# Decay rows of two half batches in own tiles, added by three-row matmuls, in a fused attention and gated FFN kernel

## Chip, cores, metric

One Trainium2 chip, one core. The metric is the device time of one execution in microseconds (us). Runs of the kernel before spread over about 1% (271.16 to 272.87 us in the first three). A run is marked slow when it is over 1.5% above the fastest run of the same kernel. The experiments ran on four chips; each run is compared with the kernel before on its own chip, in the same rounds.

## The reference, cut

```python
def _attn_ref(q, k, v, f):                     # q, k, v: (8, 8, 576, 64); f: (8, 8, 576)
    scores = scale * q @ k^T
    cum = np.cumsum(np.log(np.clip(f, 0.0001, 1.0)), axis=-1)
    decay = cum[:, :, :, None] - cum[:, :, None, :]
    scores = np.where(causal, -1e9, scores + decay)
    ... softmax ...
    return attn @ v
def _moe_ref(x, w_in, conv_w, w_out):          # x: (8, 576, 512), d_ff 1024
    h = np.maximum(x @ w_in, 0.0)
    ... three-tap convolution along the sequence, gate = sigmoid(conv) ...
    return (h * gate) @ w_out
```

The decay is of low rank. It can be added to q·k by a few additional rows in the contraction: rows that hold cum of the key beside a constant, and a constant beside cum of the query. cum is kept as a bf16 pair (high, low), which makes three rows.

## The kernel before, the parts concerned

The work is cut in 16 half batches of four heads ("hb"). q and k of a half batch lie transposed in 128-row tiles `stq`, `stk`. The decay rows are rows 96, 98 and 126 of these same tiles, so one 128-row matmul gives q·k and decay together. Before that, VectorE "clamps" each tile: one pass multiplies every row by a constant and adds another, so it can keep a row or set it to a constant. After the scores come the exponential (ScalarE), attention times V into a PSUM buffer "O" (TensorE), and a normalisation by the row sums (VectorE); V is cast to fp16 beforehand. The FFN then uses the weights W_in and W_out. The order of all instructions on every engine is fixed beforehand: the host plays through a list of tasks with estimated times and priorities (the third argument).

```python
def fill(t, p0, n, z):                  # constant rows of a tile, copied by DMA
    nc.gpsimd.dma_start(bass.AP(... n rows from p0 ...), consts[z:z + n, :])

def rows_of(hb):                        # decay rows, by DMA into the q and k tiles
    tq, tk = stq_t[hb % RING], stk_t[hb % RING]
    c = slice(hb * HH, (hb + 1) * HH)
    if hb == 1:
        nc.gpsimd.dma_start(tk[96:97, 0:HS], khi_sb[c, :])
        nc.gpsimd.dma_start(tk[98:99, 0:HS], klo_sb[c, :])
        nc.gpsimd.dma_start(tq[126:127, 0:HS], khi_sb[c, :])
        return
    ...

def scores(sc, hb, k0, q0, w, start=True, stop=True):
    nc.tensor.matmul(sc, stk_t[hb % RING][:, k0:k0 + 128], stq_t[hb % RING][:, q0:q0 + w],
                     start=start, stop=stop, skip_group_check=True)
...
            if hb:                      # q, k loaded: constant fills (GpSimd), clamp (VectorE)
                even.append(task({"POOL": 0.55 * len(rows)}, [t_fsrc, x], 2 * hb - 3.5, ... fill ...))
            if hb and (s or hb < CLAMPS):
                even.append(task({"DVE": 0.9}, [x], (2 * hb - 3 if hb > 1 else -5) + 0.2 * s, ... clamp(hb, s, 0, 4, 96)))
...
        if hb:
            t_rows[hb] = even + [task({"POOL": 1.1 if hb > 1 else 1.6}, landed, ..., rows_of(hb), lag=LANDING + 1.0)]
...
            t_norm[i] = task({"DVE": 1.05}, [t_pv[i, 1]], i - 0.0, lambda i=i: norm(i) if i else [norm(i), hold(w_in_f16)], ...)
            if i == 0:                  # W_in is loaded only after the first normalisation
                t_win = task({"POOL": 1.0}, [t_norm[0]], -0.5, ... dma_start(w_in_f16, ...) ...)
```

## Time and profile before

| | before |
|---|---|
| median of 3 runs | 271.61 us (271.16 to 272.87) |
| span of the profiled run | 271.1 us |
| TensorE busy | 241.7 us (89%), 2602 matmuls |
| VectorE / ScalarE busy | 226.9 / 212.1 us |

These are lines of the page of the kernel before: the busy share of TensorE and its granted clock in 40 slices of 6.8 us (tenths), and the group of score matmuls (count, busy us, mean ns of one, idle time before them).

```profile
PE   2864869878899999999999999999999999989990
...
PEclk9999868999999999999999999999999999999997
...
L298 PE MATMUL sc<-stq,stk 128*128 128x128 bf16 (+3 forms) x576 | 67.3, 242 | 8.1 <-ACT pm L338 3.6
```

After the start, TensorE has its gaps in slices 3 to 11 (and again at the very end), and its clock is low in slices 5 to 7. That is the stretch that the change aims at.

### The profile page before, as it was taken

What the parts mean: (1) busy time and instruction counts of PE and PEld (TensorE: products, weight loads), DVE (VectorE), ACT (ScalarE), POOL (GpSimd) and SP (SyncE); (2) the same over time, 40 slices, a digit from 0 to 9 for tenths busy, and PEclk for the clock granted to TensorE, in tenths of its full rate; (3) what the DMA queues carried; (4) which work ended last, traced back from release to release, by engine and by line L of the source; (5) the groups of instructions that cost most, each with busy time, mean ns of one, the idle gap of its engine ahead of it and who ended that gap; (6) DMA issues with size and microseconds to landing.
All of it is one profiled execution on the core that took longest, in us unless ns stands there. A gap on an engine that the chain in (4) does not pass through costs nothing.

```text
span 271.1 us, 6621 instructions
## 1 busy us (share of the span) xinstructions
PE 241.7 (89%) x2602; PEld 166.1 (61%) x2602; DVE 226.9 (84%) x401; ACT 212.1 (78%) x347; POOL 59.2 (22%) x124
## 2 busy tenths in 40 slices
PE   2864869878899999999999999999999999989990
PEld 1333646646677777776776677667776777655540
DVE  5863538999799999999989989999899999978751
ACT  5081727989879999989989899989889998577552
POOL 4491110631120340332315050406010100000000
PEclk9999868999999999999999999999999999999997
DMA  8999999999998999999999999999101201022015
GB/s 138 202 209 177 223 184 221 222 183 246 168 220 183 219 244 166 228 167 256 269 213 180 203 245 185 223 160 278 61 28 52 80 0 58 23 116 80 0 46 226
DMA packets 121284, 44.58 MB, mean 164 GB/s; under 512 B 115560, under 2 KB 116596, under 8 KB 121254
## 3 DMA queue, kind: packets, MB, share of 16 engines
q1 hardware_dynamic: 115088, 32.00, 66.9%
q0 software_dynamic: 5840, 12.01, 17.0%
q8 instruction: 20, 0.33, 0.5%
q10 hardware_dynamic: 326, 0.17, 0.4%
q14 instruction: 10, 0.08, 0.1%
HBM read 13.99 MB, written 9.58 MB: 87 GB/s over the span
## 4 chain that ended last, share of the span: by engine, by line
PE 64%; DVE 8%; DMA 7%; issue 6%; SPq 6%; ACT 5%; POOL 0%; DVEq 0%; ACTq 0%; POOLq 0%
PE mm L425 19%; PE mm L487 19%; PE sc L298 10%; PE O L356 8%; DMA stk<-in_k_dram 6%; SPq L110 5%; PE sc L330 4%; DVE u L457 2%; PE sc L500 2%; PE mm L393 2%; DVE u L455 2%; SPq L163 1%; ACT ht L438 1%; DMA out_dram<-ob 1%; ACT po L324 1%
## 5 line engine op out<-in xcount | busy, mean ns | idle before, releaser
L425 PE MATMUL mm<-xt,w_in_f 128*128 128x288 f16 x512 | 80.3, 292 | 1.7 <-DVE xt L413 0.4
L298 PE MATMUL sc<-stq,stk 128*128 128x128 bf16 (+3 forms) x576 | 67.3, 242 | 8.1 <-ACT pm L338 3.6
L324 ACT ACTIVATE po<-sc 128x1024 f16<-128x1024 f32 x64 | 64.6, 1028 | 2.6 <-PE sc L298 2.1
L438 ACT ACTIVATE ht<-mm 128x288 f16<-128x288 f32 x128 | 52.0, 414 | 12.3 <-PE mm L425 11.2
L298 PEld LDWEIGHTS <-stk 128*128 128x128 bf16 x576 | 42.4, 99 | 28.7 <-issue 7.7
L425 PEld LDWEIGHTS <-w_in_f 128*128 128x128 f16 x512 | 48.2, 100 | 18.7 <-issue 3.1
L487 PE MATMUL mm<-w_out_f,hg 128*128 128x512 f16 x248 | 58.4, 379 | 0.7 <-ACT xt L411 0.6
L455 DVE SCALAR_TENSOR_TENSOR u<-ht,cwt 128x576 f32<-128x576 f16 x64 | 51.5, 810 | 5.4 <-ACT ht L438 4.7
L457 DVE SCALAR_TENSOR_TENSOR u<-ht,cwt,u 128x576 f32<-128x576 f16 x64 | 51.5, 810 | 0.5
L475 DVE SCALAR_TENSOR_TENSOR hg<-hg,ht 128x576 f16<-128x576 f16 x56 | 41.6, 751 | 4.4 <-ACT hg L467 4.0
L467 ACT ACTIVATE hg<-u,cwt 128x576 f16<-128x576 f32 x56 | 43.4, 780 | 1.0 <-DVE u L457 0.9
L338 ACT ACTIVATE pm<-sc 128x1024 f16<-128x1024 f32 x32 | 32.9, 1028 | 11.8 <-PE sc L298 11.7
L487 PEld LDWEIGHTS <-hg 128*128 128x128 f16 x248 | 23.5, 98 | 24.2 <-issue 0.9
L356 PE MATMUL O<-va,po 128*128 128x65 f16 x640 | 36.6, 194 | 1.2 <-ACT po L324 1.0
L356 PE MATMUL O<-va,pm 128*128 128x65 f16 x256 | 31.1, 194 | 3.0 <-DVE xn L369 1.8
L356 PEld LDWEIGHTS <-po 128*128 128x128 f16 x640 | 30.5, 97 | 2.4 <-ACT po L324 1.8
L356 PEld LDWEIGHTS <-pm 128*128 128x128 f16 x256 | 24.1, 98 | 5.7 <-DVE xn L369 2.7
L369 DVE TENSOR_TENSOR xn<-O,rc 128x640 f16<-128x640 f32 x32 | 26.4, 824 | 1.1
L132 POOL DMA_DIRECT2D stq<-consts x23 | 12.2, 535 | 66.8 <-PE mm L425 27.0
L330 PE MATMUL sc<-trib,identb 128*128 128x512 bf16 x64 | 24.5, 383 | 1.2 <-ACT po L324 1.1
L511 ACT ACTIVATE ob<-mm 128x512 f32<-128x512 f32 x23 | 13.7, 598 | 11.0 <-PE mm L487 10.7
L522 POOL DMA_DIRECT2D out_dram<-ob x10 | 7.7, 768 | 44.2 <-ACT ht L438 21.9
(112 smaller groups left out, 223.8 us busy)
## 6 DMA issues: line engine op xcount, KB each, us to landing
vf<-in_v_dram SPq DMA_DIRECT2D x64, 128.0 KB, 4.0
out_dram<-ob POOLq DMA_DIRECT2D x10, 512.0 KB, 6.4
out_dram<-ob SPq DMA_DIRECT2D x10, 256.0 KB, 2.1
stq<-consts POOLq DMA_DIRECT2D x8, 216.0 KB, 4.7
vf<-in_v_dram SPq DMA_DIRECT2D x16, 64.0 KB, 5.2
w_in_f<-in_moe_w_in_dram POOLq DMA_DIRECT2D x1, 1024.0 KB, 10.7
w_out_f<-in_moe_w_out_dram POOLq DMA_DIRECT2D x4, 256.0 KB, 5.6
out_dram<-ob SPq DMA_DIRECT2D x2, 512.0 KB, 2.8
```

What stands on the lines that cost most here:

```text
L298: nc.tensor.matmul(sc, stk_t[hb % RING][:, k0:k0 + 128], stq_t[hb % RING][:, q0:q0 + w], start=start, stop=stop, skip_group_check=True)
L324: nc.scalar.activation(p_of[i, s][:, 0:1024], sc_of.pop((i, s)), AF.Exp, scale=SCALE)
L330: nc.tensor.matmul(sc[:, 512 * s:512 * (s + 1)], identb, trib, start=True, stop=False, skip_group_check=True)
L338: nc.scalar.activation(p_of[i, 2], sc_of.pop((i, 2)), AF.Exp, scale=SCALE)
L356: nc.tensor.matmul(O[:, s, 65 * Q:65 * (Q + 1)], w, va[:, h, m, :], start=(m == 0), stop=(m == Q))
L425: nc.tensor.matmul(ps[:, 0:w], w_in_f16[:, cc, 128 * ff:128 * (ff + 1)], xt[:, cc, w * t:w * (t + 1)], start=(cc == 0), stop=(cc == NCC - 1))
L438: nc.scalar.activation(ht[:, 0, HT_0 + w * t:HT_0 + w * (t + 1)], ps[:, 0:w], AF.Relu)
L455: nc.vector.scalar_tensor_tensor(u, hl, cwt[:, ff, 0:1], hc, op0=ALU.mult, op1=ALU.add)
L457: nc.vector.scalar_tensor_tensor(u, hr, cwt[:, ff, 1:2], u, op0=ALU.mult, op1=ALU.add)
L467: nc.scalar.activation(hv, u, AF.Tanh, scale=cwt[:, ff, 2:3])
L475: nc.vector.scalar_tensor_tensor(hv, hv, 1.0, hc, op0=ALU.add, op1=ALU.mult)
L487: nc.tensor.matmul(ps, chunk(g, ff, c), w_out_f16[:, ff, :], start=(ff == 0), stop=(ff == NFF - 1))
```

## The change

Its intent: half batches 1 and 2 no longer wait for decay rows in their q and k tiles. Their decay rows lie in tiles of their own, borrowed from buffers that are needed only later (V of batch 1; x^T and u), and each of their 36 score matmuls is followed by one over these three rows into the same accumulator. In addition, TensorE gets 20 matmuls of 512 columns in gaps after half batches 0 and 1, and priorities are set anew. Core of the diff (cuts marked by ...):

```diff
+    def decay_rows(hb, dk, dq):
+        dec_of[hb] = dk, dq
+        nc.gpsimd.memset(dk.bitcast(FP32), MINUS)
+        nc.gpsimd.memset(dq.bitcast(FP32), PAIR)
+    def load_decay(hb):
+        (dk, dq), c = dec_of[hb], slice(HH * hb, HH * (hb + 1))
+        nc.gpsimd.dma_start(dk[0:1, 0:HS], khi_sb[c, :])
+        nc.gpsimd.dma_start(dk[1:2, 0:HS], klo_sb[c, :])
+        nc.gpsimd.dma_start(dq[2:3, 0:HS], khi_sb[c, :])
...
+    decay_rows(1, early[0:3, 0:HS // 2].bitcast(BF16), early[0:3, HS // 2:HS].bitcast(BF16))
+    decay_rows(2, xt_pool.tile(...)...[0:3].bitcast(BF16), u_pool.tile(...)...[0:3].bitcast(BF16))
...
+    load_decay(1)
+    load_decay(2)
...
+    def warm():
+        ps = mm_pool.tile([128, 512], FP32, name="mm")
+        for t in range(2):
+            nc.tensor.matmul(ps, identb, trib, start=True, stop=True)
...
         nc.tensor.matmul(sc, stk_t[hb % RING][:, k0:k0 + 128], stq_t[hb % RING][:, q0:q0 + w],
-                         start=start, stop=stop, skip_group_check=True)
+                         start=start, stop=stop and hb not in dec_of, skip_group_check=True)
+        if hb in dec_of:
+            dk, dq = dec_of[hb]
+            n = min(128, HS - k0)
+            nc.tensor.matmul(sc[0:n], dk[0:3, k0:k0 + n], dq[0:3, q0:q0 + w],
+                             start=False, stop=stop, skip_group_check=True)
...
-    CLAMPS, HALVES, LANDING = 8, 16, 3.0
+    CLAMPS, HALVES, LANDING = 6, 8, 3.0
-    WAITS = ((3, 0), (3, 1), (4, 0), (4, 1))
+    WAITS = ((3, 1), (3, 1), (4, 0), (4, 1))
+    WARM = {0: 5, 1: 5}
...
-            t_norm[i] = task({"DVE": 1.05}, [t_pv[i, 1]], i - 0.0, ...
+            t_norm[i] = task({"DVE": 1.05}, [t_pv[i, 1]], i - 1.5, ...
...  (V loads of the next batches wait for half batch 1's scores; FFN keys, AHEAD, QUEUED set anew)
```

More of the change, by code (lines that the diff above doesn't have):

```diff
@@ L138, in rows_of @@
         c = slice(hb * HH, (hb + 1) * HH)
-        if hb == 1:
-            nc.gpsimd.dma_start(tk[96:97, 0:HS], khi_sb[c, :])
-            nc.gpsimd.dma_start(tk[98:99, 0:HS], klo_sb[c, :])
-            nc.gpsimd.dma_start(tq[126:127, 0:HS], khi_sb[c, :])
-            return
         nc.gpsimd.dma_start(tq[126:127, 0:HS], kd[0:1, c, :].rearrange("j h s -> j (h s)"))
@@ L147, in rows_of @@
                             kd[:, c, :].rearrange("j h s -> j (h s)"))
+    dec_of = {}
+    def decay_rows(hb, dk, dq):
[7 more added lines that the diff above has]
+        nc.gpsimd.dma_start(dq[2:3, 0:HS], khi_sb[c, :])
     def hold(w):
@@ L208 @@
     nc.gpsimd.tensor_copy(trv, trib[:, 0:SL].unsqueeze(1).broadcast_to((128, HH, SL)))
+    early = vf_t[1].rearrange("p h k d -> p (h k d)")
+    decay_rows(1, early[0:3, 0:HS // 2].bitcast(BF16), early[0:3, HS // 2:HS].bitcast(BF16))
+    decay_rows(2, xt_pool.tile([128, NCC, S], FP16, name="xt").rearrange("p c s -> p (c s)")[0:3].bitcast(BF16),
+               u_pool.tile([128, 2, S], FP32, name="u").rearrange("p a s -> p (a s)")[0:3].bitcast(BF16))
     nc.vector.memset(one1, 1.0)
@@ L558 @@
     last = None
+    t_dec = {hb: task({"ACT": 0.01}, [], -99, lambda: None, lag=x) for hb, x in ((1, 4.5), (2, 6.0))}
+    t_held = task({"ACT": 0.01}, [], -99, lambda: None, take="xt", also="u")
     t_fsrc = task({"DVE": 3.1}, [], -9, fill_sources)
@@ L572 @@
                 landed.append(x)
-            if hb:
+            if hb > 2:
                 t = (stq_t, stk_t)[s][hb % RING]
@@ L579 @@
             if hb and (s or hb < CLAMPS):
-                even.append(task({"DVE": 0.9}, [x], (2 * hb - 3 if hb > 1 else -5) + 0.2 * s,
-                                 lambda hb=hb, s=s: clamp(hb, s, 0, 4, 96)))
+                even.append(task({"DVE": 0.9}, [x], (2 * hb - 2 if hb > 1 else -5) + 0.2 * s,
+                                 lambda hb=hb, s=s: clamp(hb, s, 0, 4, 96 if hb > 2 else 128)))
         t_half = None
         if b == 0 and hb < 2:
-            t_half = task({"ACT": 0.01}, [], -9, lambda: None, lag=(6.5, 9.3)[hb])
+            t_half = task({"ACT": 0.01}, [], -9, lambda: None, lag=(7.5, 12.0)[hb])
             t_v[b] = t_half
         elif hb < HALVES:
-            last = t_half = task({"SP": 3.2}, [t_cast[hb - 4, p] for p in range(2)] if b >= 2 else [], key + 0.2,
+            last = t_half = task({"SP": 3.2}, [t_cast[hb - 4, p] for p in range(2)] if b >= 2 else
+                                 t_qk[1, 0] + t_qk[1, 1], key + 0.2,
                                  lambda b=b, h=HH * (hb % 2): load_v(b, h, h + HH), lag=2.3, dma=3.0, behind=last)
         elif hb % 2 == 0:
-            last = t_v[b] = task({"SP": 3.5}, [t_cast[2 * b - j, p] for j in (4, 3) for p in range(2)] if b >= 2 else [],
+            last = t_v[b] = task({"SP": 3.5}, [t_cast[2 * b - j, p] for j in (4, 3) for p in range(2)] if b >= 2 else
+                                 t_qk[1, 0] + t_qk[1, 1],
                                  key + 1.2, lambda b=b: load_v(b), lag=2.3, dma=6.0, behind=last)
@@ L596 @@
         if hb:
-            t_rows[hb] = even + [task({"POOL": 1.1 if hb > 1 else 1.6}, landed, 2 * hb - 3.6 if hb > 1 else -9 if hb > 1 else -1.0,
-                                      lambda hb=hb: rows_of(hb), lag=LANDING + 1.0)]
+            t_rows[hb] = even + [task({"POOL": 1.1}, landed, 2 * hb - 3.6, lambda hb=hb: rows_of(hb), lag=LANDING + 1.0)
+                                 if hb > 2 else t_dec[hb]]
         else:
@@ L616 @@
             exps = {}
-            x = task({"PE": 0.9}, t_rows[hb], i + 0.1, lambda i=i: diag_scores(i), take="sc")
+            x = task({"PE": 1.33 if hb in t_dec else 0.9}, t_rows[hb], i + 0.1, lambda i=i: diag_scores(i), take="sc")
             t_qk[hb, p] = [t_tail, x]
@@ L620 @@
             for s in range(2):
-                x = task({"PE": 0.46}, t_rows[hb], i + 0.2 + 0.4 * s, lambda i=i, s=s: off_scores(i, s),
+                x = task({"PE": 0.89 if hb in t_dec else 0.46}, t_rows[hb], i + 0.2 + 0.4 * s, lambda i=i, s=s: off_scores(i, s),
                          take="sc")
@@ L630 @@
                                   give=[("pm", mask)] if s else [])
-            t_norm[i] = task({"DVE": 1.05}, [t_pv[i, 1]], i - 0.0, lambda i=i: norm(i) if i else [norm(i), hold(w_in_f16)],
+            t_norm[i] = task({"DVE": 1.05}, [t_pv[i, 1]], i - 1.5, lambda i=i: norm(i) if i else [norm(i), hold(w_in_f16)],
                              take="xn" if i % PPB == 0 else None, give=[("O", t_pv[i, 0])])
@@ L635 @@
                     w_in_f16, moe_w_in.rearrange("(cc p) ff -> p cc ff", p=128)), lag=2.0, dma=6.5)
+        if hb == 2:
+            task({"ACT": 0.01}, t_qk[2, 0] + t_qk[2, 1], -9, lambda: None, give=[("xt", t_held), ("u", t_held)])
+        if hb in WARM:
+            x = None
+            for _ in range(WARM[hb]):
+                x = task({"PE": 0.44}, [t_pv[2 * hb + 1, 1], x], 999, warm, take="mm", lag=0.05)
+                gives = tasks[x][4]
+                gives.append(("mm", x))
         if hb % 2:
@@ L644 @@
             t_xt[b].append(task({"DVE": 0.3, "ACT": 0.4}, [x], i, lambda e, b=b: xpose_out(b, "t", 0, e), give=[("mm", x)]))
-    start = [PPB * (b0 + nb) + 1.0 for b0, nb in GROUPS]
-    start += [start[-1] + 4.0, start[-1] + 6.0]
+    start = [PPB * (b0 + nb) + x for (b0, nb), x in zip(GROUPS, (-1.0, 1.0, 1.5, 1.0, 1.0, 1.5, 1.5, 1.0))]
+    start += [PPB * B + 5.0, PPB * B + 7.0]
     t_exp, t_late = [], []
@@ L654 @@
         for ff in range(NFF):
-            key = start[g] + 0.8 * (start[g + 1] - start[g]) * ff / NFF
+            key = start[g] + .8 * (start[g + 1] - start[g]) * ff / NFF
             relus = []
@@ L699 @@
             t_m2.append(x)
-            x = task({"DVE": 0.62, "ACT": 0.57}, [x] + ([y] if c % 2 else []), key - 1.0,
+            x = task({"DVE": 0.62, "ACT": 0.57}, [x] + ([y] if c % 2 else []), key - 4.0,
                      lambda e, g=g, c=c: evac(g, c, e), give=[("mm", x)] if g < LAST else [], take="ob" if c % 2 == 0 else None)
@@ L709 @@
             task({"SP": 0.01}, t_m2, key, lambda: None, give=[("hg", t_hg)])
-    AHEAD, QUEUED = 3.0, 8.0
+    AHEAD, QUEUED = 8.0, 6.0
     def play():
@@ L715, in play @@
         ready = {e: [] for e in busy}
-        dma_free, clock = 21.5, 0.0
+        dma_free, clock = 23.0, 0.0
         heap, order = [], []
```

## The prediction

> **What bounds the kernel now.** I read the busy shares by stretch first, then the waits between 18 and 80 us, then the order of time of the early part engine by engine, last the DMA issues and their landings. The stretches (columns: PE, PE weight load, DVE, ACT, POOL busy us with counts, granted clock, DMA share, GB/s):
>
> ```profile
> 18.00:25.00 7.00, 3.01 (x65) 2.40 (x65) 2.38 (x7) 1.98 (x3) 3.44 (x6) 1.00 1.13 166
> 25.00:38.00 13.00, 9.80 (x128) 7.40 (x128) 7.14 (x21) 6.64 (x8) 2.03 (x4) 0.80 1.20 207
> 38.00:44.00 6.00, 5.67 (x30) 3.69 (x30) 3.20 (x7) 2.96 (x7) 0.50 (x1) 0.58 1.11 232
> 44.00:50.00 6.00, 5.69 (x77) 4.44 (x76) 5.12 (x10) 6.00 (x10) 0.79 (x2) 1.00 1.17 202
> 50.00:70.00 20.00, 15.25 (x206) 11.02 (x203) 19.86 (x36) 18.02 (x29) 8.27 (x14) 1.00 1.21 211
> 80.00:100.00 20.00, 19.93 (x226) 14.21 (x224) 18.95 (x31) 18.27 (x30) 4.75 (x9) 1.00 1.00 206
> ```
>
> There are three regimes. Up to 44 us nothing is full: TensorE waits, and from 25 to 44 us its clock is low too. From 50 to 70 us VectorE is full (19.86 of 20) and TensorE has nearly 5 us to spare. From 70 to about 250 us TensorE is full (19.93 of 20 here, the same in each later stretch up to 220 us). So what the early part loses is never made up: it pushes a nearly full pipeline to the right. Time is to be had before 70 us and nowhere else; the last 11 us (PE 4.88) are a tail that the change leaves alone.
>
> What ends the idle time early, as the order of time shows it:
>
> ```profile
> 25.07 0.28 PE L298 MATMUL sc<-stq,stk 128*128 128x64 bf16 x4 [2.69 <-DMA stq<-khi_sb]
> ```
> ```profile
> 24.72 0.43 DVE L170 TENSOR_SCALAR va<-vf 128x512 f16<-128x512 f32 x1 [3.63 <-DMA vf<-in_v_dram]
> 35.10 0.88 DVE L119 TENSOR_SCALAR stk<-stk,lim 96x2304 uint16<-96x2304 uint16 x1 [1.21 <-DMA stk<-in_k_dram]
> 36.14 0.82 DVE L369 TENSOR_TENSOR xn<-O,rc 128x640 f16<-128x640 f32 x1
> 40.97 0.82 DVE L455 SCALAR_TENSOR_TENSOR u<-ht,cwt 128x576 f32<-128x576 f16 x1 [2.69 <-ACT ht L438]
> ```
> ```profile
> 38.33 5.40 PE L425 MATMUL mm<-xt,w_in_f 128*128 128x288 f16 x24 [0.38 <-DVE xt L413]
> 43.57 0.27 PE L304 MATMUL sc<-trit,identb 128*128 128x256 bf16 x1
> ```
>
> The reader should see this. Half batch 1 had q and k clamped by 17.2 us, yet its scores start at 25.07, because its decay rows (three GpSimd DMAs, issued 18.75 to 20.65) land only then. Its last normalisation (36.14) stands on VectorE behind the clamp of half batch 2, which waits for a k that lands at 35. So the first FFN matmul is at 38.33, at half clock (24 matmuls in 5.24 us; at full clock four take 0.49, so 24 take 2.9), VectorE's first convolution is at 40.97, and half batch 2's scores are at 43.57, although its clamps ended at 35.98, again behind row DMAs issued at 35.62 and 36.13.
>
> [...] 3.01 us of work in 18 to 25 us, then 0.80 and 0.58 granted; no single gap was over 2.7 us[...]. [...] I charge the three-row matmuls by columns like the full ones. No row of this trace has a bf16 K=3; its full ones follow columns (four 128-column ones start to start in 0.22 us, so 55 ns each). [...] In this trace row DMAs of 4.5 KB took 4.9 to 5.6 us to land beside busy engines, and I use that. [...]
>
> **The change part by part.**
> *Decay by own tiles.* Removed: for half batches 1 and 2, the row DMAs into the q and k tiles and the constant fills (4 of the 38 issues that copy constants, 0.5 us of GpSimd each). Added: six row DMAs right after half batch 0's (issues from 12.6 us, 0.55 each, 3.3 us), four small GpSimd memsets (by the 512-element one at 0.53 us, some 1 us each) between 4 and 8.5 us, where GpSimd waits anyway until 10.8. With 5 us to landing, half batch 1's rows are there at about 18 to 19.5 instead of 25.07: **its scores start 5.5 us earlier.** TensorE pays: per half batch 36 more matmuls with 4x64 + 16x128 + 4x1024 = 6400 columns; at 55 ns per 128 that is 2.75 us, for two 5.5 us. Half batch 1's 2.75 lie in the hole at 18 to 25 us (4 us idle). Half batch 2's come while VectorE bounds, in the 5 us spare. So I charge nearly none of it.
>
> *What holds next.* Half batch 1's V is cast at 24.72 when its load lands; nothing moves that load forward. So: V cast to 25.7, attention-times-V of the two pairs and two normalisations (0.5 and 1.05 each, in turn, about 3.2 with latencies) to 29.5, transposes and copies 2.5, so 32. W_in was issued at 21.41 and took 10.7 to land: 32.1. Both say **first FFN matmul at about 32.5 instead of 38.33: 5.8 us.** The new normalisation priority is part of this: it no longer stands behind the clamp.
>
> *Short matmuls.* Two times five pairs of 512 columns, 20 x 0.215 = 4.3 us, placed last in priority in gaps of TensorE after half batches 0 and 1. [...] If it stays full, the first half channel needs 0.49 where it took 0.96, and the first convolution follows the first FFN matmul by 1.5 instead of 2.64 us: **1.1 us more for VectorE.**
>
> *One buffer lent.* Half batch 2's rows sit in the first buffers of xt and u until its scores end, so the first convolutions have one u buffer, not two: each waits for the tanh before it (0.78) while only the 0.75 gate can fill in. I take 0.3 us for each of three: **-1 us.**
>
> *Rest.* Clamps of q dropped for half batches 6 and 7: 2 x 0.88 us of VectorE, in the stretch where TensorE bounds: 0. Larger V loads, stores and priorities: 0 on average, with some scatter.
>
> Sum: 5.8 + 1.1 - 1.0 = 5.9, and some 1 us because half batch 2 can start at about 36.5 instead of 43.57 (it fills TensorE early, though VectorE takes most of that back). **About 7 us: 271.6 - 7 = 264.6.** Cross-check on TensorE alone: after 38.33 there are 232.8 us, of which idle 5.2 up to 80 us, 2.5 lost to the low clock, and 8.5 idle later, so 216.6 useful. 32.5 + 216.6 + 8.5 + 5 to 8 (idle and extra) + 0.5 (median over profiled span) = 263.1 to 266.1.
>
> **The rivals.** (a) *The wait moves, not the end:* V or W_in lands still later because the DMA engines are full (V's later start points in the new list hint at it), and FFN starts at 35 or 36. For it: DMA share over 1.1. Against: bytes only fall. It would make 267 to 269. (b) *VectorE is the bound and keeps its order trouble:* it is full from 50 to 70 us, and a single u buffer or a late half batch 2 stalls it in order. That would eat 2 to 4 us: 266 to 269. (c) *More than the shift:* the reordering closes TensorE's 5 us of spare at 50 to 70 us as well, since FFN of group 0 gets an earlier key and W_out and half batch 3 (whose rows GpSimd issued at 49.94, behind a W_out wait of 6.67 us) come sooner. That would make 260 to 262. (d) *A mis-set order:* matmuls placed for other landing times stall TensorE in order in the full stretch; the order is fixed and the stretch has no slack. Slower or same; the profile shows nothing for it, only the many new constants.
>
> **Range and chances.** The middle is 264.6. (c) sets the low end at 260.5, (a) or (b) the high end at 269. The 2% line is 266.2, 1.6 us above the middle and well inside the range, so faster by over 2% gets 0.66, within 2% 0.31, slower 0.03.
>
> **What the changed profile would show.** Right: half batch 1's first score matmul before 20 us; no idle of over 1.5 us on TensorE ended by a row DMA; granted clock near 1 from 25 to 44 us; first FFN matmul at 32 to 33.5 and first convolution by 34.5; half batch 2's scores by 38; then the same full stretch, TensorE over 98% busy from 70 to 240 us, only some 7 us further left; L298 with 72 more matmuls that lie in former idle time. Wrong: scores of half batch 1 still after 23 us (rows or GpSimd late); FFN after 35 us (V or W_in late); VectorE idle over 3 us behind a u buffer between 33 and 45 us; or TensorE idle in the stretch from 80 us on, which would mean that the new priorities cost or gain by themselves.

Where a cut is marked stood a passage on the hardware that no trace or run shows. The sum came to 5.8 + 1.1 - 1.0 = 5.9 us and some 1 us, about 7, so 264.6 us. Two entries are estimate alone. One is the charge for the three-row matmuls as for full ones (2.75 us per half batch, from the 55 ns read for full ones; nearly nothing in the sum, as hidden). The other is the 1.1 us, which stand only if TensorE's clock ("it" in "If it stays full") stays full: the trace shows 0.80 and 0.58 after the sparse stretch, not that short matmuls prevent this.

## The result, and the profile after

Ratios in this document are the mean time of one kernel's fast runs over that of the other's in the same rounds, so not quite the ratio of the medians quoted.

| | before, same chip | after |
|---|---|---|
| median | 272.24 us (271.16 to 273.75, 4 runs) | 300.48 us (298.1 to 303.68, 4 runs, the longest marked slow) |
| ratio | 1 | 1.1004, 95% interval 1.0901 to 1.1107 |
| TensorE busy, matmuls | 241.7 us, 2602 | 278.2 us, 2694 |

The kernel became 10% slower. These are the same lines of the page, after (a slice is now 7.5 us):

```profile
PE   3679899999987999999999999999999999989991
...
PEclk9995556855899999999999999999999999999997
...
L320 PE MATMUL sc<-stq,stk 128*128 128x128 bf16 (+3 forms) x576 | 80.9, 249 | 5.4 <-ACT pm L365 2.6
```

The early gaps are gone, but not because work moved into them profitably. TensorE is busy at half clock in slices 4 to 6, and its clock is low in 7 to 11. The table by stretch of the kernel after shows it (columns as in the prediction):

```profile
18.00:25.00 7.00, 6.01 (x39) 3.10 (x37) 1.63 (x4) 3.24 (x4) 3.71 (x21) 0.86 1.44 207
25.00:38.00 13.00, 11.83 (x90) 6.02 (x89) 2.97 (x8) 2.96 (x3) 0.86 (x1) 0.50 0.57 105
38.00:44.00 6.00, 6.00 (x45) 3.81 (x44) 2.03 (x9) 2.04 (x2) 0.00 (x0) 0.50 0.07 13
44.00:50.00 6.00, 6.00 (x44) 3.07 (x44) 1.83 (x3) 2.05 (x2) 0.00 (x0) 0.50 0.14 32
50.00:70.00 20.00, 20.00 (x112) 9.46 (x110) 4.94 (x9) 6.37 (x10) 2.05 (x4) 0.67 1.11 204
```

In 25 to 38 us TensorE finished 90 matmuls in 11.83 busy us. In the same stretch before, it finished 128 in 9.80. From 50 to 70 us it is busy all the time, yet does 112 where it did 206, while VectorE falls from 19.86 to 4.94 busy: the bound has gone from VectorE to TensorE. DMA all but stops from 38 to 50 us. How the pairs run, in order of time (start, duration; the start-to-start distance counts):

```profile
22.42 0.23 PE L320 MATMUL sc<-stq,stk 128*128 128x128 bf16 x1
...
22.58 0.23 PE L325 MATMUL sc<-vf 3*128 3x128 bf16 x1
...
22.74 0.23 PE L320 MATMUL sc<-stq,stk 128*128 128x128 bf16 x1
```

Each matmul of 128 columns, three-row or full, starts 0.16 us after the one before it (experiment 1 finds this step at full clock). Before, four such in a row took 0.22 us from start to start, 0.055 each. What follows further down:

```profile
SPq L173 <- PE sc L325: 22.2, 1, 22.2
```
```profile
29.93 0.82 DVE L396 TENSOR_TENSOR xn<-O,rc 128x640 f16<-128x640 f32 x1
...
31.08 0.86 POOL L667 DMA_DIRECT2D w_in_f<-in_moe_w_in_dram  x1 [8.88 <-DVE w_in_f L161]
...
60.14 2.10 PE L452 MATMUL mm<-xt,w_in_f 128*128 128x288 f16 x8
...
62.80 0.82 DVE L482 SCALAR_TENSOR_TENSOR u<-ht,cwt 128x576 f32<-128x576 f16 x1 [5.96 <-ACT ht L465]
```

The queue of SyncE waits 22.2 us, in one piece, for half batch 1's scores before it issues the next V load; this is the hole in the DMA share. W_in is issued at 31.08 (before: 21.41), since it hangs on the first normalisation. The first FFN matmul starts at 60.14 (before: 38.33), the first convolution at 62.80 (40.97). From 100 us on, the stretches are as full as before (TensorE 19.75 of 20 us or more up to 250 us); in 80 to 100 us TensorE is busy 17.12 us where it was 19.93. So the loss is made before 100 us.

One prediction term held in direction: half batch 1's first score matmul starts early, at 20.50 instead of 25.07 (predicted 18 to 19.5).

### The profile page after: what moved, and what is told of

The parts are those of the page before. It is cut to its first block, busy times and chain, and to the rows that moved or that the text cites. A ratio compares the mean times of both kernels' runs of the same rounds, so it can differ in the third digit from the quotient of the medians.

```text
span 299.6 us, 6761 instructions
## 1 busy us (share of the span) xinstructions
PE 278.2 (93%) x2694; PEld 179.8 (60%) x2694; DVE 226.7 (76%) x400; ACT 212.3 (71%) x346; POOL 64.5 (22%) x127
## 4 chain that ended last, share of the span: by engine, by line
PE 82%; DVE 7%; ACT 5%; DMA 2%; issue 2%; ACTq 0%; DVEq 0%
PE mm L452 20%; PE mm L514 17%; PE sc L320 16%; PE O L383 11%; PE sc L325 6%; PE sc L357 5%; PE mm L420 2%; PE sc L527 2%; ACT po L351 2%; DVE u L482 1%; PE mm L291 1%; DMA stk<-klo 1%; ACT pm L365 1%; DVE u L484 1%; DMA fsb<-in_f_dram 1%
## 5 line engine op out<-in xcount | busy, mean ns | idle before, releaser
L320 PE MATMUL sc<-stq,stk 128*128 128x128 bf16 (+3 forms) x576 | 80.9, 249 | 5.4 <-ACT pm L365 2.6
L452 PE MATMUL mm<-xt,w_in_f 128*128 128x288 f16 x512 | 81.9, 294 | 1.5 <-ACT xt L438 0.7
L351 ACT ACTIVATE po<-sc 128x1024 f16<-128x1024 f32 x64 | 65.0, 1025 | 22.2 <-PE sc L325 21.7
L320 PEld LDWEIGHTS <-stk 128*128 128x128 bf16 x576 | 44.8, 98 | 32.7 <-issue 9.9
L365 ACT ACTIVATE pm<-sc 128x1024 f16<-128x1024 f32 x32 | 32.8, 1026 | 25.7 <-PE sc L320 15.0
L383 PE MATMUL O<-va,po 128*128 128x65 f16 x640 | 39.6, 201 | 0.0
L514 PEld LDWEIGHTS <-hg 128*128 128x128 f16 x248 | 23.5, 98 | 23.7 <-issue 0.7
L383 PEld LDWEIGHTS <-po 128*128 128x128 f16 x640 | 33.3, 102 | 1.2 <-issue 0.6
L383 PE MATMUL O<-va,pm 128*128 128x65 f16 x256 | 32.9, 201 | 1.2 <-DVE w_in_f L161 1.2
L383 PEld LDWEIGHTS <-pm 128*128 128x128 f16 x256 | 25.5, 103 | 4.2 <-DVE w_in_f L161 1.3
L394 DVE RECIPROCAL rc<-O 128x10 f32<-128x10 f32 x32 | 7.0, 218 | 27.7 <-PE O L383 27.5
L357 PE MATMUL sc<-trib,identb 128*128 128x512 bf16 x64 | 25.4, 397 | 0.7 <-ACT po L351 0.5
L538 ACT ACTIVATE ob<-mm 128x512 f32<-128x512 f32 x25 | 15.0, 599 | 9.9 <-PE mm L514 9.6
```

What stands on the lines that cost most here:

```text
L351: nc.scalar.activation(p_of[i, s][:, 0:1024], sc_of.pop((i, s)), AF.Exp, scale=SCALE)
L357: nc.tensor.matmul(sc[:, 512 * s:512 * (s + 1)], identb, trib, start=True, stop=False, skip_group_check=True)
L365: nc.scalar.activation(p_of[i, 2], sc_of.pop((i, 2)), AF.Exp, scale=SCALE)
L383: nc.tensor.matmul(O[:, s, 65 * Q:65 * (Q + 1)], w, va[:, h, m, :], start=(m == 0), stop=(m == Q))
L452: nc.tensor.matmul(ps[:, 0:w], w_in_f16[:, cc, 128 * ff:128 * (ff + 1)], xt[:, cc, w * t:w * (t + 1)], start=(cc == 0), stop=(cc == NCC - 1))
L514: nc.tensor.matmul(ps, chunk(g, ff, c), w_out_f16[:, ff, :], start=(ff == 0), stop=(ff == NFF - 1))
```

## The experiments

Theory A: alternating 128-row and three-row matmuls on TensorE costs time at each change, and the few-row matmuls bring the clock down, so that the added matmuls cost some 25 us and not 5.5. Rivals: B, a three-row matmul is slow in itself, whatever stands beside it; C, the 72 more matmuls, whatever their rows, and the new priorities and order cost (with the V loads that wait). Without a letter there: D, the fills on GpSimd, the lent buffers and the short matmuls. A second question, for when A is out of the way: does the predicted shift of the FFN then come?

Summary (medians over all four runs, slow ones too; the first FFN matmul in the profiled run; "before" is 271.3 to 272.6 us median):

| run | what | median us | ratio, 95% interval | first FFN matmul, us |
|---|---|---|---|---|
| before | | 272 | 1 | 38.33 |
| after | | 300.48 | 1.1004 (1.0901 to 1.1107) | 60.14 |
| k128 | after, decay over 128 rows | 274.21 | 1.0083 (1.0028 to 1.0138) | 43.82 |
| group | after, three-row matmuls four at a time | 279.17 | one fast run: 272.39 | 40.88 |
| noown | after without own tiles | 277.38 | 1.0161 (1.0098 to 1.0224) | 37.44 |
| own3_old_quiet | before + own tiles, three rows | 302.47 | 1.1133 (1.1092 to 1.1174) | 71.01 |
| own128_old | the same over 128 rows | 275.45 | 1.0149 (1.0098 to 1.0200) | 42.20 |
| own128_hb1 | the same, half batch 1 alone | 273.66 | 1.0129 (1.0049 to 1.0210) | 38.59 |
| k128_quiet | k128, fills moved off GpSimd's early part | 270.01 | 0.9969 (0.9909 to 1.0029) | 38.51 |
| after_nowarm | after without short matmuls | 302.38 | 1.1147 (1.1095 to 1.1198) | 62.78 |
| k128_nowarm | k128_quiet without them | 276.91 | one fast run: 271.09 | 37.95 |
| k128_nowarm_hb1 | k128_nowarm, own tile for half batch 1 alone | 277.64 | 1.0222 (1.0179 to 1.0265) | 36.19 |
| k128_nowarm_win | k128_nowarm, W_in tied to a V cast | 274.55 | 1.0084 (1.0047 to 1.0120) | 36.86 |
| rows_soon | before, rows issued sooner | 276.09 | 1.0040 (0.9978 to 1.0103) | 37.27 (slow run) |
| rows_soon_norm | rows_soon, normalisations first | 274.35 | 1.0078 (1.0010 to 1.0147) | 37.30 |
| rows_soon_win | rows_soon, W_in tied to a V cast | 276.26 | 1.0130 (1.0056 to 1.0203) | 36.70 |
| rows_soon_norm_win | rows_soon with both | 276.33 | 1.0126 (1.0062 to 1.0190) | 36.10 |

### 1. The disputed cost by itself (micro)

A kernel: ten streams of bf16 matmuls on TensorE, each behind 40 full ones of 512 columns that bring the clock up (after the second stream 0.50 in 54 to 58 us, 1.00 from 60 us). Its output is wrong, which doesn't matter for the time. It ran once.

```python
for _ in range(48):  # full/3 N=128
    mm(ps[:, 0:128], wa[0:128], mv[0:128, 0:128], start=True, stop=True)
    mm(ps[:, 0:128], wb[0:3], mv[0:3, 0:128], start=True, stop=True)
# likewise: full/full, 3/3, 8 full then 8 of 3, full/32, full/64, full/65; full/3, 3/3, full/full with N=448
```

> The disputed cost by itself: ten streams of matmuls on TensorE alone, each after 40 full matmuls of 512 columns (result wrong on purpose). Theory A[...]: full/full N=128 about 55 ns a matmul; full/3 about 160 ns; 3/3 about 55 ns; eight full then eight of 3 about 55 ns plus two changes of about 105 ns in 16, so about 68 ns; full/32 and full/64 like full/3; full/65 like full/full; full/3 at N=448 about 295 ns at full clock, 3/3 at N=448 about 190. Rival B (a 3-row matmul is slow by itself[...]): 3/3 about 160 ns too, and eight/eight about 110. On the clock: if it follows the rows in use, it falls to 0.5 in 3/3 as well; if it follows the gaps, it stays 1 in 3/3[...].

The instructions of single lines, one line of each stream (count, shortest/median/longest ns, first and last start in us, form). Half the distance from first to last start, over count less one, is the mean step of a stream of two lines; the table below takes the steps of each clock apart:

```profile
L40 PE MATMUL ps<-src x96: 219/219/219, 14.7 to 25.3; 128*128 128x128 bf16 x96
```
```profile
L44 PE MATMUL ps<-src x48: 219/286/286, 34.1 to 52.8; 128*128 128x128 bf16 x48
```
```profile
L48 PE MATMUL ps<-src x64: 214/214/309, 64.9 to 74.3; 3*128 3x128 bf16 x64
```
```profile
L70 PE MATMUL ps<-src x48: 219/289/290, 186.0 to 204.3; 128*128 128x128 bf16 x48
```
```profile
L74 PE MATMUL ps<-src x48: 219/219/219, 215.6 to 221.1; 128*128 128x128 bf16 x48
```

The clock in stretches of the alternating stream (two lines) and of the one in blocks of eight (third line); the granted clock is the third number from the end, after the busy times of the engines:

```profile
34.10:38.50 4.40, 4.40 (x29) 2.52 (x27) 0.00 (x0) 0.00 (x0) 1.00 0.00 0
40.00:53.00 13.00, 13.00 (x61) 6.00 (x60) 0.00 (x0) 0.00 (x0) 0.50 0.00 1
...
85.70:92.10 6.40, 6.40 (x96) 5.26 (x95) 0.00 (x0) 0.00 (x0) 1.00 0.01 3
```

| stream | start to start at clock 1.00 | clock |
|---|---|---|
| full/full, 128 columns | 56 ns | stays 1.00 |
| full/3 | 160 ns | 0.50 after some 4.5 us, then 217 ns |
| 3/3 | 56 ns | 0.50 after some 4.4 us, then 107 ns |
| 8 full, then 8 of 3 | 16 in 1.09 us (68 ns) | stays 1.00 |
| full/32, full/64 | 160, 160 ns | falls to 0.50 |
| full/65 | 58 ns | stays 1.00 |
| full/full, 448 columns | 189 ns | stays 1.00 |
| full/3, 448 columns | 293 ns | 0.50 after some 6 us, then 483 ns |
| 3/3, 448 columns | 190 ns | 0.50 after some 3 us, then 373 ns |

Two separate costs follow. **First**, a change between 128 rows and 3, 32 or 64 rows costs some 104 ns each way (160 less 56 at 128 columns; with 3 rows 293 less 189 at 448). With 65 rows there is no such cost (58 ns). A single three-row matmul among its like costs no more than a full one (56 and 56 ns; 190 and 189). **Second**, the clock falls to half under streams of few-row matmuls although the profile shows no gap on TensorE (alternating: 4.40 busy of 4.40 us, 13.00 of 13.00; 3/3 at clock 0.50: 4.30 of 4.30). Full/65 keeps the clock. Rows times the share of time in which they stream is 0.33 at most where it fell (full/3 at 448 columns: half of (128 + 3)/128, times 189/293) and 0.42 or more where it stayed (blocks of eight: the same half, times 56/68), both estimated from this table; the runs do not show where between these the limit lies, nor that this product is the rule.

What the 104 ns consist of the runs do not show, only the time. The trace shows one thing more. In the stream of full matmuls of 448 columns the weights of a matmul are loaded one matmul ahead (0.18 us ahead). In the alternating stream each weight load starts with its own matmul (both at 102.37 us). Alternating first, then full/full (PEld is the weight load):

```profile
102.37 0.09 PEld L59 LDWEIGHTS <-src 3*128 3x128 bf16 x1 [0.20 <-issue]
102.37 0.36 PE L59 MATMUL ps<-src 3*128 3x448 bf16 x1
```
```profile
233.64 0.10 PEld L79 LDWEIGHTS <-src 128*128 128x128 bf16 x1
233.82 0.35 PE L79 MATMUL ps<-src 128*128 128x448 bf16 x1
```

So a weight load of 90 to 105 ns that nothing hides would account for the change about as well, and the change costs nearly the same at half clock (110 ns: 217 less 107, 483 less 373). No run shows whether that is the cause.

From these steps an estimate for the kernel. It has, for the two half batches, 32 pairs of 128 columns, 32 wide ones of 256 columns on average (448, 320, 192, 64), and 8 of 64. At half clock a pair costs 2 x 217 - 2 x 56 = 322 ns more than two full matmuls at full clock at 128 columns, 2 x 483 - 2 x 189 = 588 at 448, so about 430 at 256; for 64 columns I take 270. Sum: 10.3 + 13.8 + 2.2 = **26 us**. The same sum at full clock (208 ns a pair) gives 15 us. So about 15 us would be the changes and 11 the clock during them. The sum leaves out what lay in idle time and what the low clock cost all other matmuls, so a close fit is partly luck.

### 2. The same matmuls over 128 rows (k128)

```diff
-        nc.gpsimd.memset(dk.bitcast(FP32), MINUS)
+        nc.gpsimd.memset(dk.bitcast(FP32), 0.0)
+        nc.gpsimd.memset(dk[0:3].bitcast(FP32), MINUS)
-            nc.tensor.matmul(sc[0:n], dk[0:3, k0:k0 + n], dq[0:3, q0:q0 + w],
+            nc.tensor.matmul(sc[0:n], dk[:, k0:k0 + n], dq[:, q0:q0 + w],
```

> The changed kernel with the same order of work, its decay operands filled with zeros up to 128 rows, so that no matmul uses 3 rows (two more GpSimd memsets). Theory A: a full-row decay matmul costs by its columns, 2.7 us per half batch, the clock stays near 1 from 20 to 75 us, and the time is 262 to 270 us. Rival C (72 more matmuls and their order are the cost, whatever their rows): little changes, 290 to 302 us.

Measured: 274.21 us (273.63 to 276.26), ratio 1.0083, clock 0.98. The number of matmuls, their columns, the order and the priorities are those of the kernel after; only zero rows were added. Some 25 us of the 27 lost come back (1.1004 less 1.0083, of 272). That falsifies C as the main cause, since it keeps all that C blames, and fits the 26 us of experiment 1. B had fallen there already (3/3: 56 ns). The time is 4 us above the upper end of what was expected; experiment 7 finds some of that.

### 3. Three rows, but four at a time (group)

```diff
+            later.append((sc, hb, k0, q0, w, stop))     # in scores(); the three-row one is kept back
+    def flush():                                        # called after each four (or eight) full ones
+        for sc, hb, k0, q0, w, stop in later: ... the three-row matmul ...
```

> The changed kernel, 3-row matmuls kept, but the four of a bank put after its four full ones: 9 groups and 18 changes per half batch in place of 72. Theory A: the changes cost a quarter, about 12 us fewer at half clock, and more if the clock recovers: 275 to 288 us. Rival B (3-row matmuls slow by themselves): at most a few us gained, 295 to 300.

Measured: 272.39 us in the profiled run, which is fast, then 282.39, 278.46 and 279.88, all three marked slow, so there is no comparison of fast runs beyond the one (before: 272.64). The ratio, 1.0291, fits the three slow runs (mean 280.24) and not the fast one, so it is not used. Even the slowest is 18 us faster than the median after. In the profiled run the clock is 1.00 in 20 to 40 us and the first FFN matmul at 40.88. Fewer changes, without any padding, leave the clock at 1.00 as well. This separates A from B.

### 4. Everything but the own tiles (noown)

```diff
-    load_decay(1)
-    load_decay(2)
+        if hb == 1:   # rows_of as before: rows by DMA into the q and k tiles
...  new priorities, short matmuls, CLAMPS, HALVES, WAITS, AHEAD, QUEUED as after
```

> The changed kernel without the own tiles: half batches 1 and 2 get their rows by DMA as before, all the rest (short matmuls, priorities, start times) as changed. Theory A: all of the loss goes, and what is left is the worth of the rest: 266 to 273 us. Rival C (the new priorities and order cost): stays over 280 us.

Measured: 277.38 us, ratio 1.0161. So the rest of the change costs 1.6% and brings no gain (266 to 273 us were expected); it cannot be the 10%. (The V loads that wait for half batch 1's scores are not in this version; they are in k128.) Its first FFN matmul (37.44) and first convolution (39.15, before 40.97) are both earlier than before, and still it is slower.

### 5. The own tiles alone, with three and with 128 rows (own3_old_quiet, own128_old)

Priorities of before, no short matmuls; own tiles for half batches 1 and 2, filled by ScalarE (half batch 1) and late by GpSimd (half batch 2). Of the changed dependences only those stay that the lent buffers need (V loads after half batch 1's scores). The two differ only in the rows of the tiles, and so in the size of their fills:

```diff
-            nc.tensor.matmul(sc[0:n], dk[0:3, k0:k0 + n], dq[0:3, q0:q0 + w],   # own3_old_quiet
+            nc.tensor.matmul(sc[0:n], dk[:, k0:k0 + n], dq[:, q0:q0 + w],       # own128_old
```

> The own tiles of 3 rows alone, on the kernel before: its priorities, start times and load sizes, no short matmuls; the fills moved off GpSimd's early part (to ScalarE for half batch 1, later on GpSimd for half batch 2). Theory A (changes of the array's rows, 72 pairs): nearly the whole loss of the changed kernel is here too, 285 to 305 us, clock 0.5 for most of 20 to 70 us. Rival C (the new priorities and order): most of the loss is gone, 265 to 275 us.

> The same with operands filled up to 128 rows. Theory A plus the shift that was predicted: first FFN matmul at 33 to 35 us, clock near 1, 263 to 268 us. If the shift was wrong too (W_in or V set the first FFN matmul): 268 to 273 us.

Measured: 302.47 against 275.45 us, on the same chip, all runs fast: 27 us between three rows and 128. The table by stretch, first with three rows, then with 128:

```profile
20.00:40.00 20.00, 19.51 (x125) 8.94 (x124) 5.82 (x12) 4.68 (x6) 4.12 (x6) 0.55 0.74 130
```
```profile
20.00:40.00 20.00, 17.75 (x280) 14.22 (x280) 10.80 (x26) 10.87 (x14) 5.42 (x7) 1.00 1.11 202
```

With 128 rows TensorE finishes 280 matmuls in these 20 us at clock 1.00, with three rows 125 at 0.55. The 10% are made by the three-row matmuls alone, whatever the priorities, the place of the fills and the short matmuls. Also: own128_old is still 1.5% slower than before. Own tiles cost something even where their matmuls are cheap; both expectations (263 to 268, or 268 to 273) were too low.

### 6. Half batch 1 alone (own128_hb1)

```diff
-    dec_of[2] = (xt_pool.tile(...)..., u_pool.tile(...)...)
-    t_held = task({"ACT": 0.01}, [], -99, lambda: None, take="xt", also="u")     # no buffer lent
```

> The same for half batch 1 alone: no buffer of xt and u lent, 36 fewer decay matmuls, half batch 2 by DMA rows as before. If the lent u buffer and half batch 2's matmuls cost: 2 to 4 us below own128_old, 262 to 266 us. If half batch 2's early start is worth more: 1 to 4 us above it.

Measured: 273.66 us, ratio 1.0129, with one of four runs marked slow; 262 to 266 had been expected. The first FFN matmul is at 38.59, where it was before. So the lent buffers are not what eats the gain: without them it does not come either. In its trace the first normalisation comes later (23.5 to 24.6; before, 20.0 to 21.1), W_in is issued at 24.9 and lands at 35.4.

### 7. The fills off GpSimd's early part (k128_quiet)

```diff
-        nc.gpsimd.memset(dk.bitcast(FP32), 0.0)      # between 4 and 10 us, for both
+        if hb == 1:                                  # ScalarE
+            nc.scalar.mul(dk.bitcast(FP32), one1.broadcast_to((128, HS // 2)), 0.0)
+        else:                                        # GpSimd, after its other early work
+            nc.gpsimd.memset(dk.bitcast(FP32), 0.0)
```

> The changed kernel with 128-row operands as k128, but the fills moved off GpSimd's early part. If GpSimd's fills stretched VectorE's first chain (in k128 the first scores came 3.3 us later than before), they come back to about 12 us and the time falls by 3 to 4 us to 269.5 to 272 us. If that head is made up later: no change from 274.

Measured: 270.01 us (269.5 to 272.98), ratio 0.9969 with an interval over 1; k128 had 1.0083. This is the best version, and it is not shown to be faster than the kernel before. Why the fills counted is seen in order of time. The kernel after, then the kernel before:

```profile
5.23 1.05 POOL L151 MEMSET vf<- 3x1152 f32 x1
5.33 0.98 DVE L246 TENSOR_SCALAR cum<-cum,off 128x18 f32<-128x18 f32 x1
...
6.35 1.00 DVE L247 CAST khi<-cum 128x18 bf16<-128x18 f32 x1
7.26 1.08 POOL L151 MEMSET u<- 3x1152 f32 x1
...
7.38 0.18 DVE L248 TENSOR_TENSOR klo<-cum,khi 128x18 bf16<-128x18 f32 x1
```
```profile
5.45 0.23 DVE L232 TENSOR_SCALAR cum<-cum,off 128x18 f32<-128x18 f32 x1
5.72 0.18 DVE L233 CAST khi<-cum 128x18 bf16<-128x18 f32 x1
```

While GpSimd fills, a VectorE instruction over 18 elements takes 0.98 us where it took 0.23, the cast 1.00 where it took 0.18, and the clamp of q 1.18 where it took 0.57; a tensor_tensor beside the last fill (7.38 us) keeps its 0.18. This is the chain that leads to half batch 0's first scores: 13.56 us after, 12.06 before. In k128_quiet, without fills at that time, the same three take 0.24, 0.18 and 0.57 again. So tensor_scalar and casts are stretched here while GpSimd fills; by what means, no run shows. The fills moved late collide too: in k128_quiet a V cast (a tensor_scalar) takes 1.64 us at 18.66, where it took 0.29 before, while GpSimd fills up to 22.6. They are not the main hold of W_in, though: own128_hb1 has no such fills and issues W_in at 24.9.

With cheap matmuls and no such collision in the first chain the prediction's early part can be read. One line of the table by stretch, two of the order of time:

```profile
25.00:38.00 13.00, 12.75 (x201) 10.09 (x202) 7.71 (x22) 7.58 (x10) 0.86 (x1) 1.00 0.91 169
```
```profile
25.51 0.86 POOL L676 DMA_DIRECT2D w_in_f<-in_moe_w_in_dram  x1 [1.43 <-DVE w_in_f L167]
...
38.51 1.14 PE L461 MATMUL mm<-xt,w_in_f 128*128 128x288 f16 x8
```

The granted clock is 1.00 where it was 0.80, and half batch 2's scores are all but done before 38.5 (before, they started at 43.57). But TensorE is full: 12.75 of 13 us. The first FFN matmul stays at 38.51.

### 8. The short matmuls (after_nowarm, k128_nowarm)

```diff
-    WARM = {0: 5, 1: 5}
+    WARM = {}
```

> The changed kernel without its 20 short matmuls, 3-row operands kept. [...] If they only cost: 4 to 8 us below the changed kernel, 292 to 297 us. If they hold the clock anywhere that counts: 300 us or more.

> k128_quiet without the short matmuls. There TensorE is full from 25 to 44 us at clock 1, so the 20 of them (4.3 us at full clock) should count on the path: 266 to 269 us. If they lie in holes: no change, 269 to 271.

In the trace of the kernel after, two of the ten pairs run at half clock (0.83 us a pair, from 47.81 and 49.48 us; the clock is 1.00 again from 50.9 to 56 us, and 0.50 from 58 to 70), the other eight from 80.41 us on, at clock 1.00.

Measured: 302.38 us without them (all fast; after: 300.48 with a spread of 298.1 to 303.68), so in the kernel as changed they do next to nothing (the second of the two cases foreseen). In the padded version, one fast run at 271.09 and three marked slow (275.24 to 279.14), at granted clocks of 0.987 to 0.996, as high as with them. Whether they help there is not settled; if they do, it is not by the clock.

### 9. One own tile, and W_in earlier, without short matmuls (k128_nowarm_hb1, k128_nowarm_win)

```diff
+   # k128_nowarm_hb1: no own tile for half batch 2 (as in experiment 6)
-                t_win = task({"POOL": 1.0}, [t_norm[0]], -0.5, ...      # k128_nowarm_win
+                t_win = task({"POOL": 1.0}, [t_cast[0, 1]], -0.5, ...
```

> The same with own tiles for half batch 1 alone, half batch 2 by DMA rows. 36 fewer decay matmuls (2.75 us) on a full TensorE and no lent u buffer: 1 to 3 us below k128_nowarm, unless half batch 2's rows land so late that TensorE waits (then 1 to 3 us above).

> k128_nowarm with the load of W_in tied to the cast of the first V and not to the first normalisation, which half batch 1's early scores push from 21 to 25 us. If W_in's landing (33.7 us in k128_quiet) held the first FFN matmul at 38.5: it comes 2 to 4 us sooner and the time falls by 1 to 3 us. If the normalisations and transposes hold it: no change.

Measured: 277.64 (1.0222) and 274.55 us (1.0084). The first FFN matmul is at 36.19 and 36.86, 2.1 and 1.5 us earlier than before, and neither is faster. W_in, released at 21.8 us in the second, was issued only at 24.4, behind GpSimd's fills and row loads, and landed at 35.9.

### 10. The kernel before with its rows sooner (rows_soon and three more)

No added matmul at all. Half batch 1's clamps cover 128 rows, so it needs no constant fills, and its three row DMAs are issued right behind them; GpSimd's later constants are put off.

```diff
-                even.append(task({"DVE": 0.9}, [x], ..., clamp(hb, s, 0, 4, 96)))
+                even.append(task({"DVE": 0.9}, [x], ..., clamp(hb, s, 0, 4, 96 if hb > 1 else 128)))
-            t_rows[hb] = even + [task({"POOL": ...}, landed, ..., rows_of(hb))]
+            t_rows[hb] = even + [task({"POOL": ...}, landed if hb > 1 else even, ... -9.0, rows_of(hb))]
# rows_soon_norm: clamp key 2 * hb - 3 -> 2 * hb - 2, norm key i - 0.0 -> i - 1.5
# rows_soon_win:  t_win after [t_cast[0, 1]] instead of [t_norm[0]]
# rows_soon_norm_win: both
```

> The kernel before, with one thing changed: half batch 1's clamps run over 128 rows (so no constant fills for it) and its three decay row DMAs are issued by GpSimd right after them, with GpSimd's later constants put off until then. No matmul is added. Theory 1 (the prediction's chain: the rows of half batch 1 hold the early part): its first scores at 19 to 22 us instead of 25.07, first FFN matmul 2 us or more earlier than 38.3, time 267 to 269.5. Theory 2 (W_in, V and VectorE's order hold it): scores earlier, first FFN matmul within 1 us of 38.3 or later, time within 1 percent of before.

> As the run with sooner rows, and the normalisations are placed ahead of half batch 2's clamps on VectorE. If VectorE's order was the hold: first FFN matmul 1.5 to 3 us earlier than with sooner rows alone, time 266 to 269. If W_in or V is: no earlier than with sooner rows alone, since then the transposed x waits for W_in.

> As the run with sooner rows, and W_in's load follows the second V cast of half batch 0 instead of the first normalisation. If W_in was the hold: W_in landed by 32 us, first FFN matmul by 35, time 266 to 269. If VectorE's order is: W_in early, first FFN matmul still at 37 to 39 us, and time as with sooner rows alone.

> As the run with sooner rows, with both the normalisations first and W_in's load after the V cast. If the prediction's account of the early part was right but for the cost of the matmuls, this one has its first FFN matmul at 32 to 34 us and 264 to 267 us in all. If it stays at 36 us or more and within 1 percent of before, the shift was never there to be had by these means, because the DMA engines bring V, k and W_in no sooner, or the later stretch takes it back.

Measured: ratios 1.0040, 1.0078, 1.0130, 1.0126: none faster, three slower by about 1%; the times expected if the shift came, 264 to 269.5 us, were missed. In order of time with sooner rows alone (this profile is of a slow run, 278.49 us, as are two of its four; only the early part is read from it):

```profile
22.11 0.42 PE L305 MATMUL sc<-stq,stk 128*128 128x64 bf16 x4
...
34.04 0.88 DVE L119 TENSOR_SCALAR stk<-stk,lim 96x2304 uint16<-96x2304 uint16 x1 [2.13 <-DMA stk<-in_k_dram]
...
35.08 0.82 DVE L376 TENSOR_TENSOR xn<-O,rc 128x640 f16<-128x640 f32 x1
...
37.27 3.04 PE L432 MATMUL mm<-xt,w_in_f 128*128 128x288 f16 x12 [0.38 <-DVE xt L420]
```

The scores came 3.0 us earlier (22.11 instead of 25.07), the FFN 1.1. In between, the last normalisation stands behind the clamp that waits for k, as before. With both other holds taken away (rows_soon_norm_win), the normalisation is at 33.90, ahead of the clamp, W_in is issued at 21.66, 9.1 us before it lands, and the FFN starts at 36.10: 2.2 us earlier instead of 5.8. What remains is a chain that my sum left short: half batch 1's second attention-times-V waits for the normalisation of the pair before it, as there is one O buffer, and that normalisation (31.60) stands on VectorE behind the convolution weights and a copy of x^T (29.43 to 31.4). The earlier start carries far in this profile (of the fastest run, 274.00 us), and is lost late. In 44 to 50 us TensorE is busy 3.28 us, where it was 5.69, with VectorE full; but in 50 to 70 us it is busy 17.75, where it was 15.25:

```profile
44.00:50.00 6.00, 3.28 (x32) 2.14 (x30) 6.00 (x13) 4.42 (x8) 4.04 (x6) 1.00 1.24 229
50.00:70.00 20.00, 17.75 (x280) 13.94 (x278) 18.37 (x33) 19.09 (x29) 5.64 (x10) 1.00 1.33 211
```

The matmuls with W_in (512 in all), counted by the same table for their line on TensorE alone, in the first 200 us; rows_soon_norm_win first, then before (after the busy time and count stand the clock, the DMA share and GB/s):

```profile
0.00:200.00 200.00, 57.12 (x367) 0.98 1.05 198
```
```profile
0.00:200.00 200.00, 56.98 (x360) 0.97 1.09 199
```

At 100 us it is 143 against 132, at 200 us 367 against 360; at 236 us both have 448, and at 250 us the lead is gone (481 against 484). In 220 to 250 us TensorE is busy 26.95 us against 28.45; its longest wait there is 1.74 us, for ScalarE's ReLU (until 243.99).

Other versions lose their lead elsewhere: rows_soon_win has 128 at 100 us and 238 at 150 us (before: 132 and 251). That the fixed order of instructions, laid out for other landing times, causes the later idle time is likely but only argued: no run here changes that order alone.

## Why the prediction was wrong, point by point

1. **"I charge the three-row matmuls by columns like the full ones"**, 2.75 us per half batch, hidden. This is the step that failed, and it made the sign. Measured: 160 ns per matmul of 128 columns instead of 56 at full clock, 217 at half clock, and the clock at 0.50 from 25 to 50 us. In place of 5.5 us hidden, some 26 us on the path (27 between own3_old_quiet and own128_old; 25 from after to k128). The charge was an estimate that no trace had shown: it holds for three-row matmuls among their like (3/3: 56 ns), not in alternation with full ones. I had written that no row of the trace had a bf16 K=3, and gave the cost a point value all the same; none of the four rivals had this term.
2. **Half batch 1's scores from 25.07 to 18 to 19.5.** Right in direction: 20.50 in the kernel after, about 20 in k128_quiet.
3. **Fills on GpSimd "where GpSimd waits anyway".** Wrong: they stretched VectorE's first chain, and the first scores came 1.5 us later. Moving them took 1.1% off the ratio (k128 to k128_quiet; that pair also moves half batch 2's row loads).
4. **First FFN matmul at 32.5 instead of 38.33.** Wrong even where the matmuls are cheap: 36.1 to 43.8 in all such versions. W_in at 32.1 assumed its issue unmoved at 21.41. With earlier scores of half batch 1, TensorE and ScalarE come to the first normalisation later (it ends at 25.2 in k128_quiet), and W_in hangs on that. "V cast to 25.7 ... so 32" counted 3.2 us for attention-times-V and two normalisations (25.7 and 3.2 make 28.9, not the 29.5 written, a slip of 0.6 us); with W_in freed, one O buffer and VectorE's order still made it 36.10.
5. **The 1.1 us for short matmuls and a clock that stays full.** Not confirmed: no clear effect in the kernel after (300.48 against 302.38). The clock in 25 to 38 us is 1.00 without them too, in k128_nowarm and in rows_soon_win, which adds no matmul at all.
6. **One u buffer lent, -1 us.** Not resolved: own128_hb1, which lends none, is no faster than before (1.0129) and hardly faster than own128_old (1.0149).
7. **"So what the early part loses is never made up"**, so a gain there would carry to the end. Not borne out in time: seven versions without three-row matmuls have their first FFN matmul 0.9 to 2.2 us earlier than before, and none is faster. Where a profile was followed (rows_soon_norm_win), the lead passed VectorE's full stretch and lasted to about 200 us, as predicted, and was lost after it. The prediction had counted the later idle time (8.5 us) as fixed. Its "up to 44 us nothing is full" is a misreading as well: its own line has TensorE busy 5.67 of 6 us in 38 to 44, at clock 0.58.
8. **The rivals.** (d), an order that stalls, was nearest to what noown and the rows_soon versions show (+0.4 to +1.6%), but slower had a chance of only 3%. (a) and (b) name waits that exist; none of them was of the size of the loss.

What stays open: the rule by which the clock falls (it fell in streams in which the profile shows no gap, so idle time alone is not it), how much of experiment 1's split of 15 and 11 us holds inside the kernel, what the 104 ns of a change consist of, a weight load that is not hidden or something else, and what exactly makes the later idle time in the versions that start earlier.

## What to carry to other kernels

Do not put many matmuls of few rows singly between full ones (with 3, 32 and 64 rows, those tried, 160 ns each where full ones took 56, and the clock fell to 0.50): pad them with zero rows to 128, or do several in a block (68 ns in blocks of eight, clock 1.00); in this kernel 72 of them with three rows cost 27 us for the same result. Before charging a new form of an operation by its size, time it by itself in the company in which it will run, and give a form that no trace has shown a share of the range. Hidden work is hidden only if its engine is free and other engines are not slowed meanwhile (a tensor_scalar of 18 elements took 0.98 us beside a GpSimd fill, 0.23 without), and an earlier start counts only if no later wait gives it back: count finished matmuls through the whole run, and do not judge by one stretch.
